# Attention in rounds of three items beside a matmul-bound stage, with the third turn in the preparations' PSUM bank

## The chip, the cores and the metric

The kernel runs on one core of a Trainium2 chip. TensorE multiplies and transposes, VectorE (DVE) and ScalarE (ACT) read its results out of PSUM, GpSimd (POOL) does elementwise work, and SyncE (SP) issues most DMAs. Each engine works through its own queue in order; semaphores hold an instruction until what it needs is done. The metric is the device time of the whole kernel in microseconds (us), the median of several executions.

## The reference

```python
scores = scale * np.matmul(q, k.transpose(0, 1, 3, 2))     # 4 batches, 8 heads, 576 tokens, 64 wide
mask = (rel >= 0) & (rel < 128)                            # a window of 128 keys up to the query
scores = np.where(mask, scores + bias[None], -1000000000.0)
attn = np.exp(scores - scores.max(-1)); attn /= attn.sum(-1) + 1e-09
x = attn @ v                                               # rearranged to 2304 tokens x 512

P = np.exp(x @ w_gate - max)                               # 8 experts, then 8 rounds of
P /= P.sum(1) + 1e-09; P /= P.sum(0) + 1e-09; P *= N / E   #   row and column balancing
out += P[:, e:e + 1] * (np.maximum(x @ w1[e], 0.0) @ w2[e])   # e = 0..7, 512 -> 1024 -> 512

h = out @ w_in                                             # 512 -> 2048
g = np.where(h >= 1, h, np.where(h <= -1, 0.0, (h + 1) ** 2 / 4))
return g @ w_out                                           # 2048 -> 512
```

All of it is in float32. The kernel forms a float32 product as three products of rounded high and low parts (`mm3`, lines 74 to 76: high by high, high by low, low by high).

## The kernel before, in words

**Items.** Attention is cut into 80 items: 4 batches, 4 pairs of heads, and 5 blocks of queries (four of 128 and a tail of 64). A block sees its own keys and those of the block ahead of it, so block 0 has one key block and the others two. The tail's two heads share one 128-row tile.

**Steps of an item.** Each is a function, and the main loop names it by a letter.

- P, preparation (`a_prep`, three parts per pair of heads): q and k are transposed on TensorE into a PSUM tile `pst` (L290; the tails L281), ScalarE rounds it to the high part (L299), VectorE forms the low part (L302).
- S, scores (`a_scores`): products into the PSUM tiles `pss` (two banks, tags `s0` and `s1`), then on VectorE the bias, the maximum and the copy to `s` (L328).
- E, exponentials on ScalarE, one per head (L337).
- N, norm (`a_norm`): on VectorE an addition and a reciprocal of the sums (L342, L343), then the multiplication on GpSimd (L344).
- T, turn (`a_turn`): `s` is transposed by key blocks into a PSUM tile `psat` (L356). The first key block is copied to `at` by ScalarE (L360), the second by VectorE (L362).
- O, outputs (`a_out`): `at` times the values `nv` into the PSUM tile `pso` (L376); ScalarE writes the high part to `xh` (L384), VectorE the low part to `xl` (L387), which both the gate and the experts read.

**Filling.** From the first outputs on, TensorE also computes expert 0's first half (`unit0`, tiles `psg`, and the gate's logits `psl`, L396), for the tokens whose outputs are done. The main loop's letter F takes some groups of six or so of these matmuls, by a credit of `SHARE` = 1.8 for each item. What is left of it is done behind attention, in among the balancing. B advances the preparation of expert 0's weights.

**Rounds.** The order is written out by hand: a loop runs over rounds, and in each over the letters of a string. The first 20 rounds take one item each and follow `START` = "EBSNFPOT"; the 30 behind them take two and follow "ESONTPBFP". `BEHIND` says by how many items each step runs behind the scores. A list gives each part of a preparation the item from which on it may run; one is taken at each P. A value block of the next batch is loaded as soon as the last outputs that read the old one are issued; q and k of a pair of heads two ahead are loaded when a pair's third part is prepared.

**PSUM.** There are eight banks: `s0`, `s1` for scores, two for turns (`t`), one for outputs (`o`), two for filling (`g`), and one for preparations (`p`). In batch 0, two of three preparations take a filling bank.

Of the kernel before, what the change touches and what calls it, by code (L numbers as in the profile page):

```python
# [11 lines left out]
F32 = mybir.dt.float32  # L12
F32R = mybir.dt.float32r
# [6 lines left out]
P = 128  # L20
# [9 lines left out]
def attn_moe_ffn(ctx: ExitStack, tc, q, k, v, w_gate, w1, w2, w_in, w_out, out):  # L30
    nc = tc.nc
    B, H, SQ, D = q.shape
    NT, DM = out.shape
    E, _, F = w1.shape
    F2 = w_in.shape[1]
    win, wout = w_in.bitcast(U32), w_out.bitcast(U32)
    NPAIR = H // 2
# [14 lines left out]
    ps_pools = []  # L52
# [9 lines left out]
    S = {}  # L62
# [140 lines left out]
    TAIL = [slice(0, P // 2), slice(P // 2, P)]  # L203
    nat, QK, st, atT = {}, {}, {}, {}
    tails, QT = {}, {}

    def tail_at(g):
        return g if g < NPAIR else NPAIR + g % 2
# [9 lines left out]
    def a_load(g, ap):  # L218

        b, hp = divmod(g, NPAIR)  # L220
        for nm, src in (("q", q), ("k", k)):
            t = ap.tile([P, FULL, P], F32, tag=f"n{nm}", bufs=2, name=f"n{nm}")
            for j in range(2):
                sj = src[b, 2 * hp + j]
                nc.sync.dma_start(out=t[:, 0:FULL, j * D:(j + 1) * D],
                                  in_=sj[0:FULL * P, :].rearrange("(c p) d -> p c d", p=P))
            nat[g, nm] = t
        tail_load(g)

    def rows(src, b, i, h0, h1):  # L230
        x, n = QB[i]
# [26 lines left out]
        for g in range(NPAIR):  # L258
            tail_load(g)

    def a_prep(g, ap, part):

        b, hp = divmod(g, NPAIR)
        if part == 0:
            r = B - 1 - hp // 2
            for n, nm in enumerate("qk"):
                if r > b:
                    x, c0 = (xh, xl)[hp % 2], r * SQ
                    QK[g, nm] = [x[:, 2 * n + m, c0:c0 + SQ] for m in range(2)]
                else:  # L270
                    QK[g, nm] = [ap.tile([P, SQ], F32R, tag=f"{nm}{x}", bufs=3, name=f"{nm}{x}") for x in "hl"]

        if b == 0 and count[0] % 3:
            ps = ps_pools[0].tile([P, 512], F32, tag="g", bufs=2, name="pst")
        else:
            ps = ps_pools[0].tile([P, 512], F32, tag="p", bufs=1, name="pst")
        count[0] += 1
        if part == 2:
            todo = [("q", FULL, NQ, 0), ("k", FULL, NQ, P)]
            for n, nm in enumerate("qk"):  # L280
                nc.tensor.transpose(ps[:, n * P:(n + 1) * P], tails[nm, tail_at(g)], ident)  # L281
            QT[g] = [ap.tile([P, P], F32R, tag=f"qt{x}", bufs=4, name=f"qt{x}") for x in "hl"]
        elif b == 0:
            todo = [("q", 2 * part, 2 * part + 2, 0), ("k", 2 * part, 2 * part + 2, 256)]
        else:
            todo = ([("q", 0, 4, 0)], [("k", 0, 4, 0)])[part]
        for nm, i0, i1, c0 in todo if part < 2 else ():
            for i in range(i0, i1):
                x, n = QB[i]
                nc.tensor.transpose(ps[:, c0 + x - i0 * P:c0 + x - i0 * P + n], nat[g, nm][:n, i, :], ident[:n, :n])  # L290
        low = []
        for nm, i0, i1, c0 in todo:
            scale = SCALE if nm == "q" else 1.0
            s0, s1 = QB[i0][0], QB[i1 - 1][0] + QB[i1 - 1][1]
            h, l = (t[:, s0:s1] for t in QK[g, nm])
            pc = ps[:, c0:c0 + s1 - s0]
            if part == 2 and nm == "q":
                (h, l), pc = QT[g], ps[:, 0:P]
            nc.scalar.activation(h, pc, AF.Copy, scale=scale)  # L299
            low.append((l, pc, scale, h.bitcast(F32), ALU.mult, ALU.subtract))  # L300
        for x in low:
            nc.vector.scalar_tensor_tensor(*x)  # L302

    def a_scores(some, ap, bias):

        PS = [ps_pools[0].tile([P, 2, 2 * P], F32, tag=f"s{j}", bufs=1, name="pss") for j in range(2)]
        made = []
        for x, (g, i) in enumerate(some):
            q0, nq = QB[i]
            k0 = max(0, q0 - P)  # L310
            nk = q0 + nq - k0
            made.append((nq, nk, P if i == 0 else 0))
            (qh, ql), (kh, kl) = QK[g, "q"], QK[g, "k"]
            if i == FULL:
                mm3(PS[0][:, x, :nk], *QT.pop(g), kh[:, k0:k0 + nk], kl[:, k0:k0 + nk], True, True)
                continue
            for j in range(2):
                hs = slice(j * D, (j + 1) * D)
                mm3(PS[j][:nq, x, :nk], qh[hs, q0:q0 + nq], ql[hs, q0:q0 + nq], kh[hs, k0:k0 + nk], kl[hs, k0:k0 + nk],
                    True, True)  # L320
        for x, (g, i) in enumerate(some):
            nq, nk, c0 = made[x]
            h0 = 2 * (g % NPAIR)
            s = ap.tile([P, 2, 2 * P], F32, tag="s", bufs=6, name="s")
            mx = ap.tile([P, 8], F32, tag="mx", bufs=8, name="mx")
            nj = 1 if i == FULL else 2
            for j in range(nj):
                nc.vector.tensor_tensor_reduce(  # L328
                    out=s[:, j, :nk], in0=PS[j][:, x, :nk],
                    in1=bias[:, h0 + j, c0:c0 + nk] if nj == 2 else tbias[:, g % NPAIR, :], scale=-1.0,  # L330
                    scalar=3.0e38, op0=ALU.add, op1=ALU.min, accum_out=mx[:, j:j + 1])
            st[g, i] = (s, mx, nk, nj)
# [14 lines left out]
    def a_turn(g, i, ap):  # L347

        s, mx, nk, nj = st.pop((g, i))
        kbs = [i] if i == 0 else [i - 1, i]  # L350
        ps = ps_pools[0].tile([P, 2, 2, P], F32, tag="t", bufs=2, name="psat")
        at = ap.tile([P, 2, 2, P], F32, tag="at", bufs=4, name="at")
        for c, kb in enumerate(kbs):
            n = QB[kb][1]
            for j in range(nj):
# [7 lines left out]
        atT[g, i] = (at, kbs)  # L363

    def a_out(some):
        PS = ps_pools[0].tile([P, 2, P], F32, tag="o", bufs=1, name="pso")
        low = []
        for x, (g, i) in enumerate(some):
            b, hp = divmod(g, NPAIR)
# [423 lines left out]
    PREP0 = [-1, 3, 4, 0, 5, 6, 1, 7, 8, 2, 9, 10]  # L793
    PREP = [11, 14, 17, 20, 29, 34, 37, 41, 53, 56, 59, 67]
    LAG = (5, 4, 4, 5, 6, 6, 6, 6)
    with tc.manual_schedule():
        nc.gpsimd.memset(small, 0.0)
# [2 lines left out]
        make_identity(nc, ident)  # L800

        NG = B * NPAIR
        items = []
        for b in range(B):
            for c in ((0, 1), (2, 3, 4)) if b < B - 1 else (range(NQ),):
                items += [(g, i) for g in range(b * NPAIR, (b + 1) * NPAIR) for i in c]
        NI = len(items)
        preps = sorted((y, *divmod(n, 3)) for n, y in enumerate(PREP0) if n)
        preps += [(PREP[g - NPAIR] + x, g, x) for g in range(NPAIR, NG) for x in range(3)]
# [9 lines left out]
        with tc.tile_pool(name="ac", bufs=1, side="right") as ac, tc.tile_pool(name="ap", bufs=2, side="right") as ap, \  # L819
# [72 lines left out]
            while done["O"] < NI:  # L892
                s += 1
                step[0] = done["O"]
                two = new >= NSTART
                new += 1 + two
                order = ORDER if two else START
                for pos, op_ in enumerate(order):
                    some = ()
                    if op_ in done:  # L900
                        end = max(done[op_], min(new - BEHIND[two][op_], NI))
                        some = items[done[op_]:end]
                        done[op_] = end
                    if op_ == "S":
# [8 lines left out]
                        if s == 3:  # L913
                            for x in range(NPAIR, NPAIR + 2):
                                a_load(x, ap)
                        if s == 2:
                            fast.append(u0_weights(wp))
                        if s == 9:
# [5 lines left out]
                        for x in some:  # L924
                            a_norm(*x)
                    elif op_ == "T":
                        for x in some:
                            a_turn(*x, ap)
                    elif op_ == "B":
                        advance(fast, 2 * (1 + two))  # L930
                    elif op_ == "F":
                        credit += SHARE * (1 + two) / order.count("F")
                        while credit >= 1.0:
                            credit -= 1.0
                            state = next(work)
                            if state == "wait":
                                credit = 0.0
                    elif op_ == "P":
                        if s == max(PREP0) + 1:
# [120 lines left out]
```

## Time and profile before

| | us |
|---|---|
| median of 3 runs | 2061.18 |
| lowest and highest | 2060.78, 2063.77 |
| the profiled execution's own time | 2063.11 |
| its span in the trace | 2061.4 |
| TensorE busy | 2039.8 (99% of the span) |
| VectorE, ScalarE, GpSimd busy | 1222.6, 725.0, 485.6 |

The span runs from the first instruction to the last; the execution's own time is 1.7 us longer. In the trace, attention without filling lasts to about 47 us, attention with filling to about 225 us, the balancing with what is left of expert 0 to about 274 us, and the other experts with the last stage to the end. Times in the rows are microseconds from the start of the span. A matmul's end is modelled, so successive starts tell the pace better than the durations do.

### The profile page before, as it was taken

The page shows a single profiled execution, that of the slowest core. Times are in us where ns is not written, and L with a number is a line of the kernel's source. Part 1 is how long each engine was busy: PE and PEld are TensorE (multiplying, and loading weights), DVE is VectorE, ACT ScalarE, POOL GpSimd, SP SyncE. Part 2 cuts the span into 40 slices and gives each one's busy share as a digit, 9 for nine tenths or more (in the row PEclk, how much of TensorE's full clock was granted, in tenths as well). Part 3 has the DMA queues.
Part 4 walks back from the last instruction along what each step waited for, and adds up shares of the span by engine and source line. Part 5 has one row for each costly group of instructions (what it writes and reads, how often), then busy time and mean ns, then how long its engine had stood idle before and what let it go on. Part 6 is the DMA issues. An engine that isn't in the chain of part 4 may idle for free.

```text
span 2061.4 us, 30106 instructions
## 1 busy us (share of the span) xinstructions
PE 2039.8 (99%) x11071; PEld 1832.7 (89%) x11071; DVE 1222.6 (59%) x2788; ACT 725.0 (35%) x1721; POOL 485.6 (24%) x522
## 2 busy tenths in 40 slices
PE   7999999999999999999999999999999999999999
PEld 5888889989989889899899899899899898998998
DVE  5766656545545656566565665666664565656645
ACT  5776443333333332122122132222221134553543
POOL 4333437666666601111111100101110000000000
PEclk9999999999999999999999999999999999999999
DMA  7332338776776767666677566676675455555552
GB/s 154 85 84 53 137 143 293 266 265 232 264 261 234 261 223 273 235 247 237 228 247 242 209 228 237 241 259 229 228 260 180 180 191 184 197 209 183 221 189 108
DMA packets 180132, 432.83 MB, mean 210 GB/s; under 512 B 69648, under 2 KB 93712, under 8 KB 179984
## 3 DMA queue, kind: packets, MB, share of 16 engines
q1 hardware_dynamic: 168080, 411.37, 57.0%
q10 hardware_dynamic: 11904, 19.53, 3.0%
q8 instruction: 87, 1.43, 0.3%
q14 instruction: 61, 0.50, 0.1%
HBM read 311.44 MB, written 119.01 MB: 209 GB/s over the span
## 4 chain that ended last, share of the span: by engine, by line
PE 96%; DVE 2%; SPq 1%; DMA 0%; issue 0%; ACT 0%; POOL 0%; DVEq 0%; ACTq 0%; POOLq 0%
PE psg L74 16%; PE psg L76 16%; PE psg L75 16%; PE psc L74 4%; PE psc L76 4%; PE psc L75 4%; PE psd L75 4%; PE psd L74 4%; PE psd L76 4%; PE psb L74 3%; PE psa L75 3%; PE psb L75 3%; PE psa L76 3%; PE psb L76 3%; PE psa L74 3%; PE pso L376 2%
## 5 line engine op out<-in xcount | busy, mean ns | idle before, releaser
L74 PE MATMUL psg<-w2h,hh 128*128 128x512 f32 x1368 | 533.3, 390 | 0.0
L76 PE MATMUL psg<-w2h,hl 128*128 128x512 f32 x1368 | 532.8, 389 | 0.0
L75 PE MATMUL psg<-w2l,hh 128*128 128x512 f32 x1368 | 532.2, 389 | 0.0
L736 DVE SCALAR_TENSOR_TENSOR acc<-psg,pt,acc 128x512 f32<-128x512 f32 x252 | 189.1, 751 | 323.2 <-PE psg L76 321.5
L76 PEld LDWEIGHTS psg<-w2h,hl 128*128 128x128 f32 x1368 | 256.8, 188 | 53.6
L74 PEld LDWEIGHTS psg<-w2h,hh 128*128 128x128 f32 x1368 | 256.8, 188 | 50.7
L75 PEld LDWEIGHTS psg<-w2l,hh 128*128 128x128 f32 x1368 | 256.9, 188 | 50.6
L663 ACT ACTIVATE hh<-c 128x384 fp32r<-128x384 f32 x270 | 140.8, 521 | 82.2 <-DVE c L702 55.5
L665 DVE SCALAR_TENSOR_TENSOR hl<-c,hh 128x384 fp32r<-128x384 f32 x270 | 162.9, 637 | 0.0
L74 PE MATMUL psc<-xh,w1h 128*128 128x384 f32 x456 | 155.1, 340 | 1.6 <-DVE p L691 1.6
L76 PE MATMUL psc<-xh,w1l 128*128 128x384 f32 x456 | 154.9, 340 | 0.0
L75 PE MATMUL psc<-xl,w1h 128*128 128x384 f32 x456 | 154.8, 339 | 0.0
L74 PE MATMUL psd<-sh,w1h 128*128 128x384 f32 x456 | 153.3, 336 | 0.0
L75 PE MATMUL psd<-sl,w1h 128*128 128x384 f32 x456 | 153.0, 336 | 0.0
L76 PE MATMUL psd<-sh,w1l 128*128 128x384 f32 x456 | 152.9, 335 | 0.0
L684 ACT ACTIVATE p<-psa 128x384 f32<-128x384 f32 x57 | 28.0, 492 | 353.7 <-PE psa L76 351.1
L80 POOL TENSOR_TENSOR dl<-e,dh 128x128 fp32r<-128x128 f32 (+1 forms) x64 | 43.5, 688 | 363.0 <-ACT dh L79 321.0
L80 POOL TENSOR_TENSOR w2l<-raw,w2h 128x512 fp32r<-128x512 f32 x60 | 81.4, 1379 | 118.5 <-ACT w2h L79 118.5
L687 DVE TENSOR_TENSOR u<-psb,p 128x384 f32<-128x384 f32 x57 | 31.8, 557 | 114.9 <-PE psb L76 93.2
L344 POOL TENSOR_TENSOR s<-s,mx 128x512 f32<-128x512 f32 (+2 forms) x80 | 66.6, 849 | 124.2 <-DVE mx L342 77.2
L74 PEld LDWEIGHTS psc<-xh,w1h 128*128 128x128 f32 x456 | 85.7, 188 | 2.0 <-DVE p L691 2.0
L74 PEld LDWEIGHTS psd<-sh,w1h 128*128 128x128 f32 x456 | 85.7, 188 | 0.4 <-DVE c L694 0.4
(219 smaller groups left out, 4000.6 us busy)
## 6 DMA issues: line engine op xcount, KB each, us to landing
w1h<-wd1h SPq DMA_DIRECT2D x84, 896.0 KB, 4.6
w1l<-wd1l SPq DMA_DIRECT2D x84, 896.0 KB, 6.7
w2h<-wd2h SPq DMA_DIRECT2D x84, 512.0 KB, 5.2
w2l<-wd2l SPq DMA_DIRECT2D x84, 512.0 KB, 6.1
raw<-in_moe_w SPq DMA_DIRECT2D x60, 512.0 KB, 4.4
wd1h<-w1h SPq DMA_DIRECT2D x30, 896.0 KB, 6.1
wd1l<-w1l SPq DMA_DIRECT2D x30, 896.0 KB, 6.5
wd2h<-w2h SPq DMA_DIRECT2D x30, 512.0 KB, 5.9
```

What stands on the lines that cost most here:

```text
L74: nc.tensor.matmul(ps, lhsT=lh, rhs=rh, start=first, stop=False, skip_group_check=on)
L75: nc.tensor.matmul(ps, lhsT=lh, rhs=rl, start=False, stop=False, skip_group_check=on)
L76: nc.tensor.matmul(ps, lhsT=ll, rhs=rh, start=False, stop=last, skip_group_check=on)
L80: eng.tensor_tensor(l, x, h.bitcast(F32), ALU.subtract)
L344: nc.gpsimd.tensor_tensor(s[:, 0:nj, :nk], s[:, 0:nj, :nk], mx[:, 6:6 + nj].unsqueeze(2).to_broadcast([P, nj, nk]), ALU.mult)
L376: nc.tensor.matmul(PS[hs, x, :nq], lhsT=nat[b, "v", kb][:n, (2 * hp + j) * D:(2 * hp + j + 1) * D], rhs=at[:n, c, 0, TAIL[j]] if i == FULL ...
L663: nc.scalar.activation(h, c, AF.Relu)
L665: V.scalar_tensor_tensor(l, c, 0.0, h.bitcast(F32), ALU.max, ALU.subtract)
L684: nc.scalar.activation(p1, pa, AF.Copy)
L687: V.tensor_tensor(u2, pb, p1, ALU.add)
L736: nc.vector.scalar_tensor_tensor(a, ps, sc, a, ALU.mult, ALU.add)
```

## The change

The first 8 rounds still take one item, by the same string. From the ninth on there are 25 rounds, most of three items and a few of two, by "ESFeONTPB": the exponentials of the first two items, the scores, all filling of the round, the third item's exponentials, outputs, norms, turns, preparations, weights. Steps now run behind by rounds: exponentials and norms one, turns two, outputs three. The preparations of each round stand in a table, several in some rounds.

The third turn of a round takes the bank `p`. That bank also takes the scores of a round's tail item (`psf`). The preparations of these rounds take the turns' two banks, except those of batch 0 that take a filling bank. The outputs' tile holds four items. `at` has three buffers in place of four; one turn of a round takes a shorter tile (`at1`, and `s1` for its scores). The maxima `mx` have 12 buffers in place of 8. A pair's q and k are loaded at its second part, the tails at its third.

```diff
-    START, ORDER, NSTART = "EBSNFPOT", "ESONTPBFP", 20
-    BEHIND = [{"S": 0, "E": 1, "N": 1, "T": 3, "O": 4}, {"S": 0, "E": 2, "N": 2, "T": 4, "O": 6}]
+    START, ORDER = "EBSNFPOT", "ESFeONTPB"
+    BEHIND = [{"S": 0, "E": 1, "N": 1, "T": 3, "O": 4}, {"S": 0, "E": 1, "N": 1, "T": 2, "O": 3}]
     SHARE = 1.8
-    PREP = [11, 14, 17, 20, 29, 34, 37, 41, 53, 56, 59, 67]
+    PREP.update({8: [(2, 2), (3, 1)], 9: [(3, 2), (4, 0), (4, 1)], 10: [(5, 0), (5, 1)], 11: [(6, 0), (6, 1)],
...
+            elif b < B - 1:
+                steps += [[x[0][0], x[1][0], x[0][1]], [x[2][0], x[3][0], x[1][1]], [x[2][1], x[3][1]]]
+            if b < B - 1:
+                steps += [x[n][2:] for n in range(NPAIR)]
...
                     elif op_ == "T":
-                        for x in some:
-                            a_turn(*x, ap)
+                        for n, x in enumerate(some):
+                            a_turn(*x, ap, "p" if n == 2 else "t")
                     elif op_ == "F":
-                        credit += SHARE * (1 + two) / order.count("F")
+                        credit += SHARE * size
...
-                        for _, pg, x in [y for y in preps if y[0] < new][:1]:
-                            preps.pop(0)
-                            a_prep(pg, ap, x)
-                            if x == 2 and NPAIR <= pg < NG - 2:
-                                a_load(pg + 2, ap)
+                        for pg, x in PREP.get(s, ()):
+                            a_prep(pg, ap, x, "t" if two else "p")
+                            if NPAIR <= pg < NG - 2:
+                                if x == 1:
+                                    a_load(pg + 2, ap)
+                                elif x == 2:
+                                    tail_load(pg + 2)
...
-        if b == 0 and count[0] % 3:
-            ps = ps_pools[0].tile([P, 512], F32, tag="g", bufs=2, name="pst")
-        else:
-            ps = ps_pools[0].tile([P, 512], F32, tag="p", bufs=1, name="pst")
+        if part < 2 and g < NPAIR and count[0] % 3:
+            tag = "g"
+        ps = ps_pools[0].tile([P, 512], F32, tag=tag, bufs=1 if tag == "p" else 2, name="pst")
...
             if i == FULL:
-                mm3(PS[0][:, x, :nk], *QT.pop(g), kh[:, k0:k0 + nk], kl[:, k0:k0 + nk], True, True)
+                pp = ps_pools[0].tile([P, 512], F32, tag="p", bufs=1, name="psf")
+                mm3(pp[:, :nk], *QT.pop(g), kh, kl, True, True)
```

TensorE, behind the turns of a round in the second batch, before: outputs of two items (`pso`), the turns of two later ones (`psat`), one preparation (`pst`, of q), then filling.

```order
L376 MATMUL pso<-at,nv_2120 64x64 x2
L376 MATMUL pso<-at,nv_2122 64x64 x2
L376 MATMUL pso<-at,nv_2019 64x128 x2
L376 MATMUL pso<-at,nv_2118 64x128 x2
L356 MATMUL psat<-ident,s 128x128 x5
L356 MATMUL psat<-ident,s 64x128
L290 MATMUL pst<-ident,nq 128x128 x4
L74 MATMUL psg<-xh,w0h 128x384
```

TensorE at such a place now (the functions' lines have moved: L386 for L376, L366 for L356, L289 for L290):

```order
L76 MATMUL psg<-xh,w0l 128x256
L386 MATMUL pso<-at,nv_153 64x128 x2
L386 MATMUL pso<-at,nv_155 64x128 x4
L386 MATMUL pso<-at,nv_157 64x128 x2
L386 MATMUL pso<-at,nv_157 64x64 x2
L386 MATMUL pso<-at,nv_159 64x64 x2
L366 MATMUL psat<-ident,s 128x128 x9
L366 MATMUL psat<-ident,s 64x128
L289 MATMUL pst<-ident,nq 128x128 x4
L289 MATMUL pst<-ident,nk 128x128 x4
L74 MATMUL pss<-xh 128x128
```

Outputs and turns of three items stand together, two preparations follow the turns, and the next round's scores follow these; the filling has moved ahead of the outputs.

VectorE in such a round before: the low parts of the outputs (`xl`), the norms, the copies of the turns (`at`), the low part of the preparation (`kl`).

```order
L387 TENSOR_TENSOR xl<-pso,xh 128x64
L387 TENSOR_TENSOR xl<-pso,xh 128x128
L342 TENSOR_SCALAR mx<-mx 128x2
L343 RECIPROCAL mx<-mx 128x2
L342 TENSOR_SCALAR mx<-mx 128x2
L343 RECIPROCAL mx<-mx 128x2
L362 COPY at<-psat 128x256
L362 COPY at<-psat 64x128
L302 SCALAR_TENSOR_TENSOR kl<-pst,kh 128x512
```

VectorE there now (L397 for L387, L347 and L348 for L342 and L343, L372 for L362, L301 for L302; the preparations of some later pairs are kept in a free part of `xl`):

```order
L397 TENSOR_TENSOR xl<-pso,xh 128x128 x2
L347 TENSOR_SCALAR mx<-mx 128x2
L348 RECIPROCAL mx<-mx 128x2
L347 TENSOR_SCALAR mx<-mx 128x2
L348 RECIPROCAL mx<-mx 128x2
L347 TENSOR_SCALAR mx<-mx 128x1
L348 RECIPROCAL mx<-mx 128x1
L372 COPY at<-psat 128x256 x2
L372 COPY at<-psat 64x128
L301 SCALAR_TENSOR_TENSOR xl<-pst,xl 128x512
L301 SCALAR_TENSOR_TENSOR ql<-pst,qh 128x512
```

The steps keep their order; a third norm and a third copy stand ahead of the preparations.

TensorE where the first long rounds begin, ahead of all filling, before: scores of the tail (`pss<-xh,qth`), its preparation, and the outputs and turns of one item.

```order
L74 MATMUL pss<-xh,qth 128x192
L75 MATMUL pss<-xh,qth 128x192
L76 MATMUL pss<-xh,qtl 128x192
L281 MATMUL pst<-ident,tailq_117 128x128
L281 MATMUL pst<-ident,tailk_121 128x128
L376 MATMUL pso<-at,nv_151 64x128 x2
L356 MATMUL psat<-ident,s 128x128 x4
L74 MATMUL pss<-xl 128x256
```

TensorE at that place now:

```order
L74 MATMUL psf<-xl,qth 128x192
L75 MATMUL psf<-xl,qth 128x192
L76 MATMUL psf<-xl,qtl 128x192
L386 MATMUL pso<-at,nv_151 64x128 x2
L386 MATMUL pso<-at,nv_153 64x128 x2
L386 MATMUL pso<-at,nv_151 64x128 x2
L366 MATMUL psat<-ident,s 128x128 x4
L280 MATMUL pst<-ident,tailq_117 128x128
L280 MATMUL pst<-ident,tailk_121 128x128
L289 MATMUL pst<-ident,nq 128x128 x4
L289 MATMUL pst<-ident,nk 128x128 x4
L74 MATMUL pss<-xh 128x256
```

Outputs of two items now follow the scores directly, and three preparations stand together behind the turns, with no filling between them and the next scores.

## Rows read from the trace of the kernel before

**Rows 1.** The page, its first part: busy time, share of the span, instructions.

```profile
PE 2039.8 (99%) x11071; PEld 1832.7 (89%) x11071; DVE 1222.6 (59%) x2788; ACT 725.0 (35%) x1721; POOL 485.6 (24%) x522
```

**Rows 2.** Windows: stretch, length, busy time by engine, TensorE's granted clock, DMA share, GB/s.

```profile
core 0: us, PE busy (x) PEld busy (x) DVE busy (x) ACT busy (x) POOL busy (x), PEclk, DMA share, GB/s
68.60:215.90 147.30, 146.88 (x1370) 125.53 (x1368) 103.19 (x517) 105.20 (x394) 48.40 (x59) 1.00 0.29 69
274.00:2061.00 1787.00, 1781.66 (x8971) 1618.90 (x8969) 1035.31 (x1961) 556.54 (x1130) 389.46 (x400) 1.00 0.64 227
228.00:231.00 3.00, 2.07 (x14) 1.98 (x14) 0.78 (x3) 0.38 (x1) 0.03 (x1) 1.00 0.82 273
```

**Rows 3.** Waits of TensorE, 68.6 to 215.9: total us, times, longest.

```profile
PE pst L281 <- DVE kl L302: 0.4, 1, 0.4
```

**Rows 4.** Timeline of TensorE, one-item round: start, us, engine, line, operation, count.

```profile
54.86 0.65 PE L356 MATMUL psat<-ident,s 128*128 128x128 f32 x4
55.44 0.39 PE L74 MATMUL pss<-xh 64*128 64x256 f32 x2
...
55.99 0.39 PE L74 MATMUL psg<-xh,w0h 128*128 128x256 f32 x1
56.22 0.28 PE L75 MATMUL psg<-xl,w0h 128*128 128x256 f32 x1
...
56.80 0.60 PE L290 MATMUL pst<-ident,nk 128*128 128x128 f32 x4
57.33 0.66 PE L376 MATMUL pso<-at,nv 128*64 128x128 f32 x8
```

**Rows 5.** Timeline of TensorE, two-item round.

```profile
150.75 0.39 PE L74 MATMUL pss<-kh,qh 64*128 64x256 f32 x2
...
151.66 1.09 PE L376 MATMUL pso<-at,nv 128*64 128x128 f32 x16
152.68 0.87 PE L356 MATMUL psat<-ident,s 128*128 128x128 f32 x6
```

**Rows 6.** Timeline of all engines, turns of a two-item round.

```profile
147.18 1.09 PE L356 MATMUL psat<-ident,s 128*128 128x128 f32 x8
...
147.30 0.45 ACT L384 ACTIVATE xh<-pso 128x128 fp32r<-128x128 f32 x2 [0.57 <-PE pso L376]
...
147.78 0.49 DVE L387 TENSOR_TENSOR xl<-pso,xh 128x128 fp32r<-128x128 f32 x2
...
148.11 0.60 PE L290 MATMUL pst<-ident,nq 128*128 128x128 f32 x4
148.18 0.14 DVE L342 TENSOR_SCALAR mx<-mx 128x1 f32<-128x1 f32 x1
...
148.70 0.73 DVE L362 COPY at<-psat 128x256 f32<-128x256 f32 x2
```

**Rows 7.** Timeline of all engines, turns of a one-item round.

```profile
57.91 0.65 PE L356 MATMUL psat<-ident,s 128*128 128x128 f32 x4
58.03 0.28 ACT L384 ACTIVATE xh<-pso 128x128 fp32r<-128x128 f32 x1
...
59.08 0.42 DVE L362 COPY at<-psat 128x256 f32<-128x256 f32 x1
```

**Rows 8.** Timeline of all engines, turns with the latest copy.

```profile
85.07 0.88 PE L356 MATMUL psat<-ident,s 128*128 128x128 f32 x6
...
87.13 0.40 DVE L362 COPY at<-psat 128x256 f32<-128x256 f32 x1
```

**Rows 9.** Timeline of all engines, two preparations close together; in brackets idle time before, releaser.

```profile
127.03 0.69 DVE L302 SCALAR_TENSOR_TENSOR kl<-pst,kh 128x512 fp32r<-128x512 f32 x1
...
127.77 0.33 PE L281 MATMUL pst<-ident,tailq 128*128 128x128 f32 x1 [0.38 <-DVE kl L302]
```

**Rows 10.** Timeline of ScalarE, an exponential ahead of all filling.

```profile
42.90 0.50 ACT L337 ACTIVATE s<-s,mx 128x256 f32<-128x256 f32 x1
```

**Rows 11.** The values' tiles, 60 to 230: issue to landing.

```profile
DMA to landing us min/median/max: 2.9/4.1/5.4
```

**Rows 12.** Timeline of TensorE behind attention.

```profile
229.02 0.44 PE L396 MATMUL psl<-xh,wgs 128*128 128x384 f32 x1 [0.93 <-DVE hl L481]
```

More of the change, by code (lines that the diff above doesn't have):

```diff
@@ L205, in attn_moe_ffn @@
     tails, QT = {}, {}
+    short = []
     def tail_at(g):
@@ L259, in first_load, with a_prep @@
             tail_load(g)
[L261 removed]
+    def a_prep(g, ap, part, tag="p"):
         b, hp = divmod(g, NPAIR)
@@ L281, in a_prep @@
                 nc.tensor.transpose(ps[:, n * P:(n + 1) * P], tails[nm, tail_at(g)], ident)
-            QT[g] = [ap.tile([P, P], F32R, tag=f"qt{x}", bufs=4, name=f"qt{x}") for x in "hl"]
+            QT[g] = [ap.tile([P, P], F32R, tag=f"qt{x}", bufs=3, name=f"qt{x}") for x in "hl"]
         elif b == 0:
@@ L304, in a_scores @@
     def a_scores(some, ap, bias):
-        PS = [ps_pools[0].tile([P, 2, 2 * P], F32, tag=f"s{j}", bufs=1, name="pss") for j in range(2)]
-        made = []
-        for x, (g, i) in enumerate(some):
+        PS = [ps_pools[0].tile([P, 512], F32, tag=f"s{j}", bufs=1, name="pss") for j in range(2)]
+        made, c1 = [], 0
+        for g, i in some:
             q0, nq = QB[i]
@@ L365, in a_out @@
     def a_out(some):
-        PS = ps_pools[0].tile([P, 2, P], F32, tag="o", bufs=1, name="pso")
+        PS = ps_pools[0].tile([P, 4, P], F32, tag="o", bufs=1, name="pso")
         low = []
@@ L802, in attn_moe_ffn @@
         NG = B * NPAIR
-        items = []
+        steps = []
         for b in range(B):
-            for c in ((0, 1), (2, 3, 4)) if b < B - 1 else (range(NQ),):
-                items += [(g, i) for g in range(b * NPAIR, (b + 1) * NPAIR) for i in c]
+            x = [[(b * NPAIR + n, i) for i in range(NQ)] for n in range(NPAIR)]
+            if b == 0:
+                steps += [[x[n][i]] for n in range(NPAIR) for i in range(2)]
+            elif b < B - 1:
+                steps += [[x[0][0], x[1][0], x[0][1]], [x[2][0], x[3][0], x[1][1]], [x[2][1], x[3][1]]]
+            if b < B - 1:
+                steps += [x[n][2:] for n in range(NPAIR)]
+            else:
+                steps += [[x[0][0], x[0][1], x[1][0]], x[0][2:], [x[1][1], x[1][2], x[1][4]],
+                          [x[1][3], x[2][0], x[3][0]], [x[2][1], x[2][2], x[2][4]], [x[2][3], x[3][1], x[3][4]], x[3][2:4]]
+        NSTART = 2 * NPAIR
+        items = [x for y in steps for x in y]
         NI = len(items)
-        preps = sorted((y, *divmod(n, 3)) for n, y in enumerate(PREP0) if n)
-        preps += [(PREP[g - NPAIR] + x, g, x) for g in range(NPAIR, NG) for x in range(3)]
+        for y in steps[2 * NPAIR:]:
+            short.extend([x for x in y if x[1] in (0, FULL)][-1:])
+        until = [sum(len(y) for y in steps[:x + 1]) for x in range(len(steps))]
         blocks = [(7, 0, 256), (19, 256, 256), (27, 512, 256), (39, 768, 384), (47, 1152, 256), (59, 1408, 256),
@@ L894, in attn_moe_ffn @@
                 step[0] = done["O"]
-                two = new >= NSTART
-                new += 1 + two
+                two = s >= NSTART
+                size = len(steps[min(s, len(steps) - 1)])
+                new = until[min(s, len(steps) - 1)]
                 order = ORDER if two else START
                 for pos, op_ in enumerate(order):
-                    some = ()
+                    some, part = (), 0
+                    if op_ == "E" and two:
+                        part = 2
+                    op_ = op_.upper()
                     if op_ in done:
-                        end = max(done[op_], min(new - BEHIND[two][op_], NI))
+                        end = s - BEHIND[two][op_]
+                        end = max(done[op_], until[min(end, len(steps) - 1)] if end >= 0 else 0)
+                        if op_ == "O":
+                            end = min(end, done["T"])
+                        if op_ == "N":
+                            end = min(end, done["E"])
+                        if part:
+                            end = min(end, done[op_] + part)
                         some = items[done[op_]:end]
```

42 lines of the change are left out of this document (26 added, 16 removed), and 4 rows, old and new, of the table PREP.

## The prediction

> **What bounds the kernel now.** I read the page first, then the windows by stage, then the waits of TensorE, and last the timelines of single rounds. The page says that TensorE is busy for 99% of the span [rows 1]. The windows say where this holds [rows 2]: from 68.6 to 215.9 us, attention with filling, TensorE is busy for 146.88 of 147.30 us, while VectorE has 103.19 and ScalarE 105.20; from 274 us to the end, 1781.66 of 1787.00. The change doesn't touch the code behind attention, so its whole effect lies before 274 us. There TensorE has almost nothing left to lose to waits: in the long attention stretch the waits name one, of 0.4 us [rows 3]. So the change can gain only by making the same matmuls pass in less time, and it loses whatever new waiting it brings. TensorE executes the same matmuls before and after; only their order differs.
>
> **What a longer round saves.** Each change from one kind of work to the next costs TensorE something that doesn't grow with the items. A one-item round [rows 4, 7] and two two-item rounds [rows 5, 6] give it. Scores take 0.55 us for one item (55.44 to 55.99) and 0.91 for two (150.75 to 151.66): 0.36 an item, 0.19 fixed. Outputs take 0.58 for 8 products (57.33 to 57.91) and 1.02 for 16 (151.66 to 152.68): 0.14 fixed. Four transposes of turns take 0.58 (54.86 to 55.44) and eight 0.93 (147.18 to 148.11): 0.09 each, 0.23 fixed. Six filling products of 256 columns took 0.81 (55.99 to 56.80), the last five of them 0.58, so 0.11 fixed. Together 0.67 us a round. Beside filling there were 12 rounds of one item and 30 of two; now there are 25. 17 x 0.67 = 11 us gained. Preparations that now stand behind turns and no longer behind filling, where four of them took 0.53 (56.80 to 57.33), are more of the same kind there and may cost only their 0.09 each; that could add 1 to 2 us, which I leave in the range.
>
> **What the banks cost.** The first two turns of a round take the two turn banks, the third takes the bank that the preparations had for themselves, and the preparations of these rounds now take the turn banks. They come right behind the turns on TensorE, so a round's first preparation has to wait until ScalarE and VectorE have copied the round's first turn out. VectorE's copy is the late one: ahead of it stand the low parts of the outputs, which wait for ScalarE's high parts, and the sums and reciprocals of the norms. The two-item round shows the chain [rows 6]: turns start at 147.18, the two high parts run to 147.75, the two low parts from 147.78, the two norms from 148.18, the copies at 148.70; two take 0.73 and one alone 0.4 [rows 8], so the first is out at about 149.10, 1.92 us after the turns began. A third item adds a high part (0.45 for two against 0.28 for one [rows 6, 7]: 0.17), a low part (half of 147.78 to 148.18: 0.20) and a norm (half of 148.18 to 148.70: 0.26). That makes 2.55. Ten transposes last 0.23 + 10 x 0.09 = 1.1 us. So TensorE waits 1.45 us, and so do all the scores and the filling behind the waiting transposes in its queue. The second preparation waits for the second copy, some 0.35 later, which the first one's four transposes (4 x 0.09 = 0.36) cover.
>
> In the order, 22 of the 25 rounds have a preparation. Three of these have no filling yet and are counted below; in four the first turn has no VectorE copy (block 0 has one key block, copied by ScalarE, which is early enough). 15 are left: 15 x 1.45 = 21.8 us. The trace shows this wait only in miniature, so it gets bounds. The shortest lag to the end of VectorE's copy is that of a one-item round, 57.91 to 59.50 = 1.59 [rows 7]; less 1.1 that is 0.48, or 7.2 us in all. The longest is 85.07 to 87.53 = 2.46 in a two-item round [rows 8]; with 0.63 for the third item 3.1, a wait of 2.0, or 30 us. I take 21.8, from the two-item round in which nothing was late: its length is a chain of dependent steps, so a third item can hardly shorten it. What a prepared bank that is held up does is seen once in the stretch: at 127.77 the tail's transposes waited 0.38 us for a split on VectorE [rows 9], which is the one wait of [rows 3].
>
> The Trainium skill (page "Perfetto Trace Analysis", section "Optimization Strategy") says that the same gap repeating on the engine that should be saturated can mean too little PSUM for the next tile. The wait at 127.77 agrees in kind, and by that rule the change makes one such gap a regular one; it gives no price, so the sum is unchanged.
>
> **The start.** Filling still waits for the first outputs, so the first three of the new rounds have none. In a round of two plain items (two exponentials each) and a tail (one), ScalarE has five exponentials of 0.5 [rows 10], 0.6 of high parts, three copies that I put at VectorE's 0.4 [rows 8] and two splits at VectorE's 0.69 [rows 9], 5.7 us; TensorE has 0.19 + 3 x 0.36 = 1.3 of scores, 1.0 of outputs, 1.1 of turns and 8 x 0.09 = 0.7 of preparation, 4.1. That is 1.6 us of idling each and some 4 us over the three, since the first enters with work done ahead. Bounds: 0, if this lead lasts, and 8, if the outputs' wait for ScalarE and the preparations' wait for VectorE add up.
>
> **The rest.** In three rounds the scores use a preparation made just ahead of them. A split ends some 2.0 us after its transposes begin (148.11 to 148.70 + 0.73 + 0.69 [rows 6, 9]); the scores' queue covers more than half of it, and I put what is left at 0.4, 0.75 and 1.0 us by what stands between in the order: some 2.5 us with a little for a fourth place, between 0 and 6. The tail's scores now take the third turn's bank; in the last rounds, where no preparation gives it time, some 0.9 us once. The loads of q and k come one step earlier and are hidden as before. Value loads at three batch boundaries have about one round, 5 us or more, against 4.1 us to land, at most 5.4 [rows 11]: hidden, at worst 0.5 us each. More buffers for the maxima and shorter tiles for some turns cost no instruction.
>
> **Sum.** -11 + 4 + 21.8 + 2.5 + 0.9 = +18.2 us on the profiled execution's 2063.11, 2081.3. That execution lies 1.9 us above the median of the runs, 2061.18 (2060.78 to 2063.77), so in terms of the median 2079.
>
> **Rivals.** *Faster: the wait hides.* If VectorE reached the first copy within the 1.1 us of the turns, only the gain and the start would be left: 2061.2 - 11 + 4 = 2054. It decides if the lag falls under about 1.1 us. For it: VectorE is busy for 70% of the stretch, and the filling now stands ahead of the outputs, so that it may enter them with nothing left over. Against: the 1.92 us of [rows 6] hold no foreign work. Chance 0.12.
>
> *No change: half a wait.* With the lag of the one-item round, 0.48 a wait, the terms are -11 + 4 + 7.2, 2061.4. For it: that row. Against: it needs three items to be as quick as one. Chance 0.10.
>
> *Slower by far: the clock.* Idling in every round could lower TensorE's clock from 2.4 to 1.2 GHz. If it did so in the 15 waiting rounds of some 6.5 us, they would take twice as long: about +100 us, 2180. In this trace the granted clock stayed at 1.00 over an idle time of 0.93 us at 229 [rows 2, 12], somewhat shorter than those expected. Chance 0.03. The Trainium skill (page "TensorE: Matmul & The Clock Gate", section "A second HAM failure mode: psum-queue depth-cycling") tells of a kernel whose clock oscillated because PSUM banks were cycled with short idle times between groups of matmuls; the idle time of [rows 12] doesn't bear that out, but it doesn't repeat.
>
> **How the numbers follow.** The forecast, a wait of about 1.45 us in most rounds, has 0.75. Its own range comes from the bounds: -11 + 0 + 7.2 = 2057 at the least, -11 + 8 + 30 + 6 = 2094 at the most, and from the two lags that I think likely, 1.0 and 1.8 us, 2070 to 2086. The range for 8 in 10 reaches down into the no-change case: 2059 to 2090; it leaves the faster rival, the clock, and a few in a hundred of the long waits outside. A change of less than 0.2% (4.1 us) can't be told from none here. Faster by more: the first rival and a little of the second, 0.13. Within: most of the second, and the low edge of the forecast, 0.12. Slower: 0.75.
>
> **What the profile after would show.** If right: idle time of TensorE ahead of preparation transposes behind turns, of about 1.2 us as shown (the last transposes' modelled end hides some 0.2 to 0.3 of a wait), ended by VectorE's copy of a turn, in some 15 rounds; idle time of some microseconds ahead of outputs or turns between 43 and 55 us; runs of scores, turns and outputs fewer and longer, filling right behind the scores; the stage from 274 us on as long as before, shifted by 15 to 20 us. The first step is wrong if these idle times are under half a microsecond or are ended by another engine; the gain is wrong if the stretch is longer by more than its idle time says. A granted clock under 1.00 in attention would mean the third rival, and idle time ahead of outputs ended by a DMA, the value loads.

## The result and the profile after

The changed kernel takes 2085.36 us (median of 4 runs, 2085.28 to 2088.85) against 2060.98 for the kernel before (2060.70 to 2063.77): 24.4 us slower, a ratio of 1.0119 with a 95% interval of 1.0102 to 1.0137. The forecast was 2079, with 2059 to 2090 as the range.

The windows say where it lies. The first two are attention and balancing, from the span's start to the first matmul of the next stage, of the kernel before and of the changed one; the third is the rest of the changed kernel. Columns as in [rows 2].

```profile
0.00:274.82 274.82, 258.92 (x2105) 214.49 (x2106) 188.03 (x831) 168.46 (x591) 96.10 (x122) 1.00 0.40 99
```

```profile
0.00:297.28 297.28, 256.34 (x2108) 214.58 (x2108) 185.86 (x832) 166.01 (x591) 95.68 (x122) 0.99 0.37 92
...
296.00:2083.00 1787.00, 1782.17 (x8972) 1619.09 (x8970) 1035.34 (x1956) 556.63 (x1130) 387.88 (x400) 1.00 0.63 227
```

The later stage is as long and as busy as in [rows 2]. Ahead of it TensorE is busy 2.6 us less and idle 25.0 us more (40.94 against 15.90), which makes the 22.5 us of this stretch. What it waited for from 52 to 250 us, where the kernel before has three waits of 1.6 us in all, those of [rows 3] and [rows 12] among them (total us, times, longest; the longest lines):

```profile
PE pst L289 <- DVE at L372: 12.0, 10, 1.5
PE pst L280 <- DVE at L372: 5.7, 5, 1.3
PE psf L74 <- DVE at L372: 1.0, 2, 0.8
PE psl L406 <- ACT o L507: 0.7, 1, 0.7
PE pss L75 <- DVE kl L301: 0.7, 2, 0.4
PE pss L75 <- DVE xl L301: 0.5, 1, 0.5
```

These are fifteen waits of preparations (L289, and L280 for tails) for VectorE's copy of a turn, 17.7 us as shown. One of them, in the timeline of all engines of a three-item round, answers to [rows 6]:

```profile
115.06 1.31 PE L366 MATMUL psat<-ident,s 128*128 128x128 f32 x10
115.18 0.56 ACT L394 ACTIVATE xh<-pso 128x128 fp32r<-128x128 f32 x3 [1.25 <-PE pso L386]
115.78 0.62 DVE L397 TENSOR_TENSOR xl<-pso,xh 128x128 fp32r<-128x128 f32 x3 [1.69 <-ACT xh L394]
...
116.31 0.15 DVE L347 TENSOR_SCALAR mx<-mx 128x2 f32<-128x2 f32 x1
...
117.10 0.92 DVE L372 COPY at<-psat 128x256 f32<-128x256 f32 x3
117.56 0.66 PE L289 MATMUL pst<-ident,nk 128*128 128x128 f32 x4 [1.18 <-DVE at L372]
```

VectorE's copy stands behind ScalarE's high parts, its own low parts and the norms (116.31 to 117.10, 0.26 each), and only then comes the preparation, 2.50 us after the turns began. VectorE stood idle for 1.69 us ahead of the low parts: it isn't short of time, it gets the work late.

Ahead of the filling, from 27 to 52 us:

```profile
PE pst L289 <- DVE at L372: 3.4, 2, 2.6
PE psat L366 <- DVE mx L333: 1.7, 1, 1.7
PE pso L386 <- DVE xl L397: 0.6, 1, 0.6
PE pst L280 <- ACT at L370: 0.5, 1, 0.5
```

That is 6.2 us, where the kernel before idled 0.5.

### The profile page after: what moved, and what is told of

Read it like the earlier page. It is cut to its first block, busy times and chain, and to the rows that moved or that the text cites. A ratio compares the mean times of both kernels' runs of the same rounds, so it can differ in the third digit from the quotient of the medians.

```text
span 2083.6 us, 30051 instructions
## 1 busy us (share of the span) xinstructions
PE 2037.2 (98%) x11071; PEld 1832.6 (88%) x11071; DVE 1221.2 (59%) x2788; ACT 722.6 (35%) x1721; POOL 483.6 (23%) x522
## 3 DMA queue, kind: packets, MB, share of 16 engines
q8 instruction: 87, 1.43, 0.3%
## 4 chain that ended last, share of the span: by engine, by line
PE 93%; DVE 4%; SPq 1%; ACT 1%; issue 1%; DMA 0%; POOL 0%; DVEq 0%; ACTq 0%; POOLq 0%
PE psg L74 16%; PE psg L76 16%; PE psg L75 16%; PE psc L74 4%; PE psc L76 4%; PE psc L75 4%; PE psd L75 4%; PE psd L74 4%; PE psd L76 4%; PE psb L74 3%; PE psa L75 3%; PE psb L75 3%; PE psb L76 3%; PE psa L76 3%; PE psa L74 3%; PE pso L386 2%
## 5 line engine op out<-in xcount | busy, mean ns | idle before, releaser
L74 PEld LDWEIGHTS psg<-w2h,hh 128*128 128x128 f32 x1368 | 256.8, 188 | 50.8 <-DVE acc L746 0.3
```

Of the source, the lines that this page charges most:

```text
L74: nc.tensor.matmul(ps, lhsT=lh, rhs=rh, start=first, stop=False, skip_group_check=on)
```

## The experiments

Each time is a median, with the ratio to the kernel before run on the same chip (2060.9 to 2061.2 in the three groups).

**Norms behind the turns.** 

> The changed kernel with the order ESFeOTNPB: the norms stand behind the turns, so VectorE copies the turns out before it does the three sums and reciprocals (0.26 us each). Theory (bank wait): the first preparation waits for VectorE's copy of the first turn, whose chain is high parts, low parts, norms, copy; without the norms it is 0.78 us shorter. 15 waits of about 1.4 us become 0.6: 15 x 0.78 = 11.7 us less, about 2073.5, with 15 waits left that show 0.3 to 0.5 us. Rival (the waits only show where time is lost anyway, and the longer rounds themselves cost it): within 2 us of 2085.4. If in addition the clock stays up at 68.7 us, 3.4 less.

```diff
-    START, ORDER = "EBSNFPOT", "ESFeONTPB"
+    START, ORDER = "EBSNFPOT", "ESFeOTNPB"
```

2071.45 us (2069.21 to 2073.04), ratio 1.0048 (1.0033 to 1.0063): 13.9 us less than the changed kernel. Waits of TensorE, 52 to 250 us:

```profile
PE pst L289 <- DVE at L372: 4.6, 10, 0.7
PE pst L280 <- DVE at L372: 1.7, 4, 0.5
```

Idle time of TensorE up to the next stage fell from 40.94 to 26.83 us. The shown waits went from 17.7 to 6.3, by 11.4; 11.7 were expected from 0.78 a wait. Six instructions of 0.15 us moved behind the copies shorten each wait by what they last: the chain on VectorE sets it.

**Filling between turns and preparations.** 

> The changed kernel with the order ESeONTFPB: the filling stands between the turns and the preparations. The banks are shared as before, but some 3.7 us of filling pass between a turn and the preparation that takes its bank. Theory (bank wait): the 15 waits of 1.4 us vanish, 21 us less, and with them the 6.8 us of half clock at 68.7 us, 3.4 less: 2061 to 2064. What then is left against the kernel before is the start less the gain of fewer rounds. Rival 1 (the third item's bank, its shorter tiles or the longer rounds cost the time): 2080 or more. Rival 2 (late filling lets the outputs wait for ScalarE's exponentials instead): idle time ahead of outputs or turns of 0.5 to 1 us in each round, 2072 to 2085.

```diff
-    START, ORDER = "EBSNFPOT", "ESFeONTPB"
+    START, ORDER = "EBSNFPOT", "ESeONTFPB"
```

2062.91 us (2059.56 to 2066.15), ratio 1.0008 (0.9998 to 1.0017): 22.4 less than the changed kernel, and the same as the kernel before. Of the 15 waits one of 0.22 is left. What TensorE waits for from 52 us on, the longest lines:

```profile
PE pscs L440 <- DVE small L436: 1.1, 2, 0.8
PE pss L75 <- DVE kl L301: 0.9, 3, 0.4
PE psl L406 <- ACT o L507: 0.7, 1, 0.7
```

So neither the third item nor the shared banks as such cost the time, but a preparation so close behind the turn whose bank it takes. And with 25 rounds for 42 the time is the same, so what the longer rounds gain is no more than what else they cost.

**Batch 0 in one-item rounds.** 

> The changed kernel with all of batch 0 (20 items) in one-item rounds as in the kernel before, and the rounds of three from batch 1 on. Theory of the start: the three long rounds without filling cost some 8 us (filling starts 4.7 us later although the clock rose 14 us earlier in that profile); they go, two of the 15 waits go too (2.8 us), 8 rounds more cost 8 x 0.67 = 5.4: 2079 to 2080; 3.4 less if the half clock at 68.7 us, which followed such rounds, goes too, so 2076. Rival (a later start of the filling costs nothing, as its matmuls are only shifted): 2085.4 + 5.4 - 2.8 = 2088.

```diff
+            if b == 0:
+                steps += [[x[n][i]] for n in range(NPAIR) for i in range(2, NQ)]
-        NSTART = 2 * NPAIR
+        NSTART = 5 * NPAIR
...
```

The table of preparations is written anew to match. 2087.36 us (2085.37 to 2092.82), ratio 1.0130 (1.0114 to 1.0147). My expectation didn't come true; 2088, the rival's, did. The idle time of 27 to 52 us did go:

```profile
PE pst L280 <- DVE mx L333: 0.9, 1, 0.9
PE psf L74 <- DVE xh L301: 0.3, 1, 0.3
```

It is 1.2 us in place of 6.2. But TensorE is busy for 265.31 of its 298.86 us here, 9.0 more than in the changed kernel. A part is eight rounds more, a part the clock: in this execution the matmuls kept half the pace up to 41.6 us and again from 79.2 to 82.6, in the changed kernel's up to 27.7 and from 68.7 to 75.5. (The later stretches show a granted clock of 0.50; for the first ones the windows print 1.00, and the half pace is read from the matmuls' starts.) The two can't be told apart by this run, so the start's price isn't settled by it.

**Both.** 

> Both edits: batch 0 in one-item rounds, and from batch 1 on the order ESeONTFPB. Theory: waits gone (21), start gone (8), 8 rounds more (5.4), half clock gone (3.4): 2058 to 2061, at or a little below the kernel before (2061.0), since 21 rounds of three stand for 30 of two: 9 x 0.67 = 6 us gained less what the scores still wait for fresh preparations. Rival: 2065 or more, if three-item rounds have another cost.

2068.12 us (2064.35 to 2069.34), ratio 1.0026 (1.0015 to 1.0038), above what I expected, inside the rival's 2065 or more, and above the run with the late filling alone. The late filling took 19.2 us off here as well. Its first waits were a preparation's of 2.9 us and an output's of 1.0 ahead of all filling, so one-item rounds aren't free of them either.

**Twenty more one-item rounds in the kernel before.** 

> The kernel before with 40 instead of 20 one-item rounds: 20 items that were taken by two are taken by one, which makes 10 rounds more and changes no bank. It measures what a round costs apart from its items. Theory of the prediction (0.67 us fixed per round, 0.17 more where a preparation stands between filling and outputs): 10 x 0.67 to 0.84, +7 to +8 us, 2068 to 2069. Rival (the fixed cost was taken too high: the sums by kind of work put rounds of three at some 3 us less than the 17 x 0.67 = 11 of the prediction, about 0.2 a round): +2 to +3 us, 2063 to 2064.

```diff
-    START, ORDER, NSTART = "EBSNFPOT", "ESONTPBFP", 20
+    START, ORDER, NSTART = "EBSNFPOT", "ESONTPBFP", 40
```

2069.06 us (2065.99 to 2069.81), ratio 1.0035 (1.0023 to 1.0048): 8.2 more for 10 rounds, 0.8 each. The traces tell it more closely. Up to the first filling product of `psg` the kernel before, this run and the run with both edits take the same one-item rounds in the same order, so the stretch from there to the next stage compares what follows: the kernel before, this run, both edits (columns as in [rows 2]).

```profile
50.45:274.82 224.37, 220.62 (x1885) 187.76 (x1884) 159.43 (x704) 139.47 (x491) 71.84 (x83) 1.00 0.32 87
47.14:277.52 230.38, 226.91 (x1885) 187.93 (x1884) 162.10 (x704) 141.12 (x491) 72.37 (x83) 1.00 0.31 84
51.42:277.08 225.66, 219.10 (x1885) 189.56 (x1884) 158.74 (x703) 135.07 (x490) 70.68 (x83) 1.00 0.31 86
```

Twenty rounds of one in place of ten of two cost 6.0 us, 0.60 for each round more; between rounds of two and of one the cost is about what I took, though the one-item rounds also follow the other string. But 21 rounds of three in place of 30 of two, with the late filling, saved only 1.5 us of TensorE's busy time, some 0.17 a round (the modelled ends hide a little of each wait, so it may be somewhat more), and 2.8 us more of idling took that back.

**Filling between outputs and turns.** 

> The changed kernel with the order ESeONFTPB: filling between outputs and turns. VectorE does low parts and norms during the filling, and only the copies follow the turns; preparations stand right behind the turns again. Theory: the first copy is out about 1.0 us after the turns begin, which last 1.07, so the wait is 0 to 0.3 us instead of 1.4: 16 to 21 us less; and the preparations need no switch of their own from filling, some 2 us less than in the run with filling behind the turns (2062.9): 2059 to 2064. Rival (the low parts of the filling's results stand ahead of the copies on VectorE): waits of 0.5 to 1 us remain, 2067 to 2074.

```diff
-    START, ORDER = "EBSNFPOT", "ESFeONTPB"
+    START, ORDER = "EBSNFPOT", "ESeONFTPB"
```

2074.25 us (2071.58 to 2076.04), ratio 1.0061 (1.0047 to 1.0075): the rival's 2067 to 2074, but not by its cause. The shown waits of preparations fell from 17.7 to 7.2 us. Timeline of all engines, a round:

```profile
113.21 1.25 PE L366 MATMUL psat<-ident,s 128*128 128x128 f32 x10
...
113.51 0.41 DVE L491 SCALAR_TENSOR_TENSOR hl<-psg,hh 128x256 fp32r<-128x256 f32 x1
113.91 0.93 ACT L370 ACTIVATE at<-psat 128x256 f32<-128x256 f32 x3 [1.13 <-PE psat L366]
114.33 0.99 DVE L372 COPY at<-psat 128x256 f32<-128x256 f32 x3 [0.41 <-ACT at L370]
114.81 0.66 PE L289 MATMUL pst<-ident,nk 128*128 128x128 f32 x4 [0.34 <-DVE at L372]
```

The filling's low part was done at 113.92. VectorE then waited 0.41 us for ScalarE's copy of the same turn, which itself began 0.70 after the turns. With nothing else ahead of it, a turn's bank is free 1.60 us after the turns began, still more than the turns last.

**The start's preparations in the filling's banks.** 

> As the run before, and in the three long rounds ahead of all filling the first two preparations take the filling's banks, which are idle there. Theory of the start: the waits of preparations at 42.8 (2.6 us) and 49.9 (0.8) go, up to 3.4 us less than with the filling in the middle alone. Rival (TensorE then waits for ScalarE or VectorE at the next outputs or turns): within 1 us of it.

```diff
-                        for pg, x in PREP.get(s, ()):
-                            a_prep(pg, ap, x, "t" if two else "p")
+                        for n, (pg, x) in enumerate(PREP.get(s, ())):
+                            a_prep(pg, ap, x, ("g" if s < 11 and n < 2 else "t") if two else "p")
```

2073.49 us (2069.80 to 2074.88), ratio 1.0055 (1.0043 to 1.0068): the rival's result, within 1 us of the run before. Waits of TensorE, 27 to 52 us:

```profile
PE psat L366 <- DVE mx L333: 2.7, 1, 2.7
PE pso L386 <- DVE xl L397: 2.1, 1, 2.1
PE psat L366 <- DVE xh L301: 0.6, 1, 0.6
```

The preparations' waits of 3.3 us are gone and 5.4 stand ahead of turns and outputs. At the start VectorE is behind, whatever bank is used.

**The changed kernel once more.** 

> The changed kernel as it is, profiled once more: shows whether the clock rises and falls at the same places in another execution. If the fall at 68.7 us is caused by the idling there, it is there again; if it is the chip's own time grid, it lies elsewhere. The 15 waits stand at the same places by either, within 0.1 us each.

2087.84 us in one run. The same 15 waits are there, of 0.83 to 1.52 us, each within 0.02 us of the first execution's, and again a stretch at half the clock in the round at 70 us; the last section has its rows. But the granted clock was also 0.50 from 33.8 to 40.6 and from 50.8 to 54.2 us, where the first execution has none: not every fall is at a fixed place.

**Other banks, same order.** 

> The changed kernel with its order and its rounds, but other banks: the third turn takes a filling bank, a round's first preparation the bank p again, its second a filling bank, a third a turn bank, and the tail's scores a turn bank. Nothing moves in any engine's order. Theory (bank wait): the 15 waits of preparations for VectorE's copies (1.19 us shown, about 1.4 each) go; in their place the filling may wait for a filling bank by up to 0.4 us: 15 to 21 us less than 2085.4, 2064 to 2070. Rival (the wait is one for VectorE's backlog, whichever bank is used): it moves to the filling, idle time of about 1 us ahead of psg, 2080 or more.

```diff
-                            a_prep(pg, ap, x, "t" if two else "p")
+                            a_prep(pg, ap, x, "pgt"[n] if two else "p")
...
-                            a_turn(*x, ap, "p" if n == 2 else "t")
+                            a_turn(*x, ap, "g" if n == 2 else "t")
...
-                pp = ps_pools[0].tile([P, 512], F32, tag="p", bufs=1, name="psf")
+                pp = ps_pools[0].tile([P, 512], F32, tag="t", bufs=2, name="psf")
```

2074.44 us (2072.62 to 2076.86), ratio 1.0063 (1.0050 to 1.0075): 10.9 less, half of what I expected. Waits of TensorE, 52 to 250 us:

```profile
PE pst L289 <- DVE at L372: 6.1, 5, 1.5
PE pst L280 <- DVE at L372: 2.8, 2, 1.5
```

Eight of the 15 waits are gone, with every instruction in its place; 8 x 1.4 is 11. That this meets the 10.9 so closely is in part luck, since the stretches at half the clock differ as well (last section). Seven waits are left. One of these, all engines:

```profile
112.75 0.60 PE L366 MATMUL psat<-ident,s 128*128 128x128 f32 x4
113.19 0.60 PE L289 MATMUL pst<-ident,nk 128*128 128x128 f32 x4
...
114.07 0.92 DVE L372 COPY at<-psat 128x256 f32<-128x256 f32 x3
...
115.05 0.66 PE L289 MATMUL pst<-ident,nq 128*128 128x128 f32 x4 [1.27 <-DVE at L372]
```

The first preparation, in its own bank, follows the turns at once; the second, in a filling bank, waits for the last of three copies, the third turn's. A possible reason, which I haven't tried, is that an unfinished group of filling holds the other filling bank there, so that the third turn and the second preparation get the same one. In the eight rounds it was the bank and not VectorE's backlog: where the bank differs the wait is gone.

**Rounds of two from the ninth and from the fifteenth on, in the kernel before.** 

> The kernel before with rounds of two items from the ninth round on (8 one-item rounds in place of 20): 6 rounds fewer, with the banks and the order of two-item rounds as they are. By the run with 20 more items in one-item rounds (8.2 us for 10 rounds) 6 rounds are worth 5 us; two to three rounds stand ahead of all filling and may lose 1 to 3 us there: 2057 to 2060, a little under the kernel before. Rival (rounds of two cannot be fed so early, ScalarE and VectorE are behind): 2061 to 2064.

> The kernel before with 14 one-item rounds in place of 20: 3 rounds fewer, all beside filling, which has begun by then. 3 x 0.8 = 2.4 us less: 2058 to 2059. Rival (rounds this early wait for ScalarE): within 1 us of the kernel before.

The edits set `NSTART` to 8 and to 14 (the first also has a pool of tiles opened only once, as a long round has two P). 2064.54 us (2063.12 to 2066.19), ratio 1.0015 (1.0006 to 1.0024), just above the first rival's range; and 2060.69 (2059.58 to 2063.60), ratio 0.9997 (0.9988 to 1.0006), the second rival's. With rounds of two from the ninth on, a tail's preparation waits 2.5 us for VectorE at 49 us. From the fifteenth on, TensorE is busy 1.1 us less from the first filling product to the next stage (219.54 against 220.62) but idles 0.9 more (4.63 against 3.75); new there are two waits of preparations, 0.4 us for VectorE and 0.7 that the profile puts down to no engine. The expected 2.4 us didn't come. No version tried beats the kernel before.

## Why the prediction was right, and where its sizes were off

The step that decided it was right in kind, place, number and size: a round's first preparation waits for VectorE's copy of the round's first turn, in 15 rounds. The chain was put at 2.55 us and is 2.50 (115.06 to 117.56); ten turns were put at 1.1 and last 1.07 (next rows), so a wait is 1.43 against 1.45, and 15 are 21.5 us against 21.8. As shown they are 1.18 on average, as forecast, nine of them 1.18 to 1.20 and the others between 0.83 and 1.52. Shortening the chain and putting filling in between took off what this says; changing banks took off eight waits where all 15 were expected to go. The Trainium skill's sentence on consistent bubbles (page "Perfetto Trace Analysis", section "Optimization Strategy") was the right warning: there are 15 gaps of about one size, and with other PSUM banks eight of them are gone.

The term that was mis-sized is the gain of longer rounds, "17 x 0.67 = 11 us gained". The waits (21.5), the start (+5.7), and scores that wait for fresh preparations and for the bank `p` (2.4, against 3.4 forecast) make 29.6 us; the clock took some 3.5 back, an estimate: the matmuls came to full pace 14 us earlier in this execution than in that of before (27.7 against 41.6) and fell once to half for 6.8 us, so they were slow for 7 us less, and half of that is saved. 26.1 less 22.5 leaves a gain of about 4. The run with the late filling, where these waits are gone, agrees: TensorE is busy for 253.76 us up to the next stage against 258.92, 5.2 us less, of which some 1.6 goes to slow stretches that were 3.3 us shorter (up to 34.9 and from 45.2 to 48.6 us). Its timeline of TensorE shows one mistake in the working:

```profile
138.50 1.09 PE L366 MATMUL psat<-ident,s 128*128 128x128 f32 x8
139.35 0.36 PE L74 MATMUL psg<-xh,w0h 128*128 128x256 f32 x1
...
144.36 1.31 PE L366 MATMUL psat<-ident,s 128*128 128x128 f32 x10
145.43 0.36 PE L74 MATMUL psg<-xh,w0h 128*128 128x256 f32 x1
```

Eight turns ahead of filling take 0.85 and ten 1.07, 0.11 each and nothing fixed. I had set four turns that were followed by scores ([rows 4]) against eight that were followed by more transposes ([rows 6]) and read the difference as 0.23 fixed. What a switch costs depends on what follows, so blocks can be compared only with the same follower. That can account for up to 17 x 0.23 = 4 of the 7 us that are missing. The larger mistake was to carry a price found between rounds of one and of two over to rounds of three. The three windows with the run of 20 more one-item rounds put it at 0.60 us a round between one and two items, but at some 0.17 between two and three, in the order with the late filling. Of the 17 rounds saved, 8 are in batch 0, from rounds of one, and 9 behind it, from rounds of two: 8 x 0.60 + 9 x 0.17 is 6 us, an estimate, in place of 11 and above the 4 that the balance leaves. Why a third item saves so little no run shows.

The start was put at 4 us and idled 5.7 more than before. Its cause was put down to ScalarE's and VectorE's work without filling, and the runs agree: taking the bank waits away there only moved them. But 5.7 isn't the price of the long rounds alone. Two other runs take the first 14 rounds or more as the kernel before does and came to full pace by 28 us, as the changed kernel did (20 more one-item rounds; rounds of two from the fifteenth on): they idled 3.5 and 2.7 us in the same stretch, in rounds that their edits don't touch. The kernel before, at half pace up to 41.6, idled 0.5. At about equal pace the long rounds add nearer 3 us. What the start costs in the end I can't say to better than a few us, since its slow stretches differ from one execution to the next by as much.

The rival of the clock came true in small: one fall in the profiled execution, worth some 3.4 us, and three falls, 17 us in all, in the second; not 100 us. Value loads showed no wait behind the first outputs. The median moved 24.4 us where the profiled executions differ by 22.2 (2085.28 against 2063.11), because the one of before lay 2.1 above its median.

## What to carry to other kernels

When two uses share a PSUM bank, write down for each pair in order how long the reader in between needs from the first writer's start, and put at least that much other TensorE work between them; moving the filling there recovered 22 of the 24 us here, and moving the norms off the reader's chain some 14. The gain from longer runs of one kind need not go on as it began: here a round more cost 0.60 us between one and two items and 0.17 between two and three. Size it from blocks of the length in question, with the same neighbours.

## What the runs showed that I had not expected

TensorE's clock fell to half in the same round in both executions of the changed kernel. Windows of the first (columns as in [rows 2]; the granted clock is the third number from the end):

```profile
66.00:67.00 1.00, 0.40 (x4) 0.40 (x5) 0.96 (x5) 0.00 (x0) 1.00 (x2) 1.00 0.00 0
67.00:68.00 1.00, 1.00 (x13) 0.83 (x11) 0.14 (x2) 0.70 (x2) 1.00 (x2) 1.00 0.00 0
68.00:69.00 1.00, 0.51 (x5) 0.22 (x3) 1.00 (x2) 1.00 (x3) 0.41 (x2) 0.85 0.53 122
69.00:70.00 1.00, 0.73 (x7) 0.73 (x8) 0.22 (x1) 1.00 (x7) 1.00 (x1) 0.50 0.94 214
...
72.00:75.00 3.00, 3.00 (x17) 2.78 (x15) 0.90 (x5) 1.36 (x5) 0.00 (x0) 0.50 0.00 0
75.00:76.00 1.00, 1.00 (x15) 1.00 (x16) 0.00 (x0) 0.00 (x0) 0.00 (x0) 0.74 0.00 0
```

And of the second:

```profile
71.00:72.00 1.00, 0.39 (x1) 0.20 (x1) 0.96 (x2) 1.00 (x5) 0.41 (x2) 0.65 0.73 167
72.00:74.00 2.00, 1.99 (x13) 1.77 (x14) 0.41 (x3) 1.17 (x7) 0.99 (x1) 0.50 0.79 179
74.00:78.00 4.00, 4.00 (x20) 3.78 (x21) 1.64 (x11) 1.36 (x5) 0.00 (x0) 0.50 0.00 0
78.00:79.00 1.00, 1.00 (x20) 0.97 (x18) 0.00 (x0) 0.00 (x0) 0.00 (x0) 0.94 0.00 0
```

The clock, at 2.4 GHz from 27.7 us until then, went to 1.2 GHz at 68.7 us, behind a preparation's wait of 1.19 us and one of 0.25 in the scores, and just ahead of one of 0.5. It came back 6.8 us later, most of them unbroken work. The other 14 waits, of about the same length, brought no fall in either execution.

The place, where the scores wait 0.2 to 0.26 and 0.4 to 0.5 us for a preparation made just ahead of them, had a fall in four other versions too, of 3.4 us each: norms behind the turns, batch 0 in one-item rounds, filling between outputs and turns, other banks. It had none in three: the late filling, both edits, and the start's banks, though this last has the same waits there as the run with the filling between outputs and turns. So a fall is frequent at this place, and what decides it the runs don't show. With the other banks the clock fell at 78.7 us too, behind a single wait of 1.50, and at 126.5, behind one of 0.85.

The Trainium skill (page "TensorE: Matmul & The Clock Gate", section "A second HAM failure mode: psum-queue depth-cycling") tells of a clock that oscillates over short idle times between groups of matmuls; these rows agree in kind for one round of 25, where three such times came close together, and not for the other 14 waits. The forecast's chance of 0.03 was for a fall in all 15 rounds; one fall of 6.8 us is a term of some 3 us in the sum.
